# A layer-norm, linear-attention and MLP sum on one core: the MLP pair with the half chunk is moved to the front of the second pass

## The chip, the core and the metric

The kernel runs on one core of a Trainium2 chip. A core has a matrix engine (TensorE, PE in the profile, with PEld for its weight loads), a vector engine (DVE), a scalar engine (ACT), a general engine (POOL) and a queue engine (SP) from which this kernel issues nearly all its transfers; 16 DMA engines move the data. The metric is the device time of one execution in microseconds (us).

## The reference

The input `x` has 2048 tokens of 640 values. Everything is float32.

```python
xn = layernorm(x)
# A: linear attention, 32 heads of 20
q, k, v = split(xn @ wqkv)
phi(z) = concat(softmax(z @ w_phi), softmax(-(z @ w_phi)))      # per head, 40 features
o   = phi(q) @ (phi(k).T @ v) / (phi(q) @ sum(phi(k)) + 1e-6)
A   = o @ wo
# B: MLP, hidden width 1728
B   = gelu(layernorm(xn) @ w1 + b1) @ w2 + b2
out = x + A + B
```

## The kernel before, in words

The tokens are cut into four blocks of 512. A float32 operand is split exactly into a high and a low part, and a product of two operands is three matmuls (`mm3`, lines 69 to 72): high by high, high by low, low by high. The hidden width 1728 is cut into chunks of 128: 13 full ones and a half one of 64. Two chunks make a pair, so there are six full pairs, 0 to 5, and pair 6, which is a full chunk and the half one.

The stages in order of time are:

- The first MLP pass takes all pairs over blocks 0 and 1 (`passes`, line 289). Its sums `acc[0]` and `acc[1]` are stored to `a_dram`.
- The projections of all 16 token tiles, the features of q and k, and the sum over `phi(k)` and `v` (loop at line 1017). The output weights `wo` are split here and stored as `wo_dram`, high and low. The phi of q are stored to `e_dram` (`store_phi`).
- The second MLP pass takes all pairs over blocks 2 and 3. Beside it runs the attention of all four blocks (`attend`, line 1314): its steps are handed out one at a time at each `tick()`, which the code of the MLP calls after each group of matmuls. For a block there are 11 groups of heads, each with a load `e`, a high part on ACT (line 1207), a low part on POOL (1208) and two matmuls (1214, 1215); then `quotients` (line 1235), which stores denominators, loads them as `dt`, takes a reciprocal on DVE (1247), spreads it as `rx` with shuffles on DVE (1263) and multiplies on POOL (1265).
- The output projection (line 1410): 4 blocks x 5 row groups x 15 matmuls. It adds the sums `acc` and stores.

A pair is computed in one of two ways. `passes` takes one block at a time: 15 matmuls per full chunk and block, 10 for the half chunk (whose high and low halves share one weight tile), so 60 for a full pair over two blocks and 50 for pair 6. `cross` (line 414) takes both blocks at once by a scheme with seven block products instead of eight: 7 x 6 matmuls, and 4 x 3 for the fifth slice of the inputs, 54 in all. For it the raw weights are combined on POOL (`sums`), and combined inputs `t2`, `t3`, `t4` lie in `tf0` and `tf1`; the even slices of y[3] are overwritten by `t1`. Inside `cross` the second product of the pair before, `before`, is advanced in five pieces. `second` (line 334) is a pair's second product for one block: five groups of 6 matmuls in three PSUM banks (5, 6, 7), each followed by an add to `acc` on DVE (line 342).

In the second pass before the change pair 0 goes by `passes`, pairs 1 to 5 by `cross`, and pair 6 by `passes` again; for pair 6 the overwritten slices of y[3] are loaded back (line 1385). While pair 6 runs, the output weights are loaded into places `w2` and `w0` (`load_wo`, line 1292), block 0's attention output `ob` into `tf0` and, after it, block 1's into `tf1`, and block 0 is split into high and low parts (`first_split`, line 1301).

The order on TensorE, DVE, ACT and POOL in the second pass is that of the code from line 1358 on; on SP, and on DVE, ACT and POOL before that line, a scheduler sets it when the program is built, and SP issues its transfers in that order and waits before each one for what it needs.

Of the kernel before, what the change touches and what calls it, by code (L numbers as in the profile page):

```python
# [51 lines left out]
def tile_kernel(ctx: ExitStack, tc: tile.TileContext, x, xT, wkT, wqT, wv, wphi, wo, w1, b1, w2, b2,  # L52
# [161 lines left out]
    class Mlp:  # L214
        def __init__(self, slots, hid):
            self.hid, self.turn, self.slots, self.beside, self.raw = hid, 0, slots, iter(()), {}
            self.ph, self.px, self.po = Banks(0, 1, 2), Banks(3, 4), Banks(5, 6, 7)
            self.due, self.ticks = [], 0
# [70 lines left out]
        def passes(self, g, b, ws, hid=None):  # L289
# [7 lines left out]
            for j, (w1h, w1l, w2h, w2l) in enumerate(todo):  # L297
                gt = gts[:, j, :512]
                hs = mtile(self.hid[self.turn][j], F32R)
                hh, hl = hs[:, 0, :512], hs[:, 1, :512]  # L300
                if not (g == 6 and j == 1):
                    self.first(g, j, b, ws[j], gt, hh, hl)
                    hid.append((hh, hl))
                else:
                    pz = self.ph()
                    for kc in range(KC):
                        nc.tensor.matmul(pz, w1h[:, kc, :], yh[:, kc, :], start=kc == 0, stop=False)  # L307
                        nc.tensor.matmul(pz, w1l[:, kc, :], yl[:, kc, :], start=False, stop=kc == KC - 1)  # L308
# [5 lines left out]
                    nc.gpsimd.tensor_tensor(hh[64:128, :], gt[0:64, :], f(hh[0:64, :]), op=ALU.subtract)  # L314
                    hid.append((hh, None))
            yield
            for m in range(KC):
# [10 lines left out]
                if g == 0:  # L328
                    nc.vector.scalar_tensor_tensor(acc[b][:, m, :], pw, b2t[:, m:m + 1], acc[b][:, m, :], op0=ALU.add, op1=ALU.add)
                else:  # L330
                    nc.vector.tensor_tensor(acc[b][:, m, :], pw, acc[b][:, m, :], op=ALU.add)  # L331
# [26 lines left out]
        def take_pair(self, g, second, slot):  # L358
# [158 lines left out]
    mlp = Mlp((0, 1, 2, 3), ((0, 2), (1, 3)))  # L517
# [499 lines left out]
    for t, i in [(t, i) for t in range(14) for i in range(4)] + TAIL:  # L1017
# [35 lines left out]
        if (t, i) == (11, 0):  # L1053
            mlp = Mlp((0, 3, 2, 1), ((1, 2), (0, 3)))
            mlp.ph = ptile
            mlp.fetch_pair(0, False)
        if (t, i) == (12, 3):
            with tc.issue_after(evac):
                w1t, parts = mlp.take_pair(0, False, 0)
                for part in parts:  # L1060
                    part()
            mlp.fetch_pair(0, True)
        if (t, i) == (15, 3):
            w2t, late = mlp.take_pair(0, True, 3)
# [3 lines left out]
    mlp.fetch_pair(1, False)  # L1068
# [33 lines left out]
    before = mlp.passes(0, 2, ws)  # L1102
# [59 lines left out]
    class Attention:  # L1162
# [108 lines left out]
        def split(self, c, eng):  # L1271
# [15 lines left out]
            if c == KC and b < 2:  # L1287

                acc[b] = tfp.tile([P, KC, 512], F32, name=f"tf{b}")
                nc.sync.dma_start(acc[b], a_dram[b])  # L1290

    def load_wo():

        for p, wd in enumerate(wo_dram):
            w = wp.tile([P, 4, D], F32R, name=f"w{(2, 0)[p]}")
            nc.sync.dma_start(f(w), wd[:, 0:4, :])
            last = rp.tile([P, D], F32R, name=f"r{1 + p}")
            nc.sync.dma_start(f(last), wd[:, 4, :])
            wol.append([w[:, kc, :] for kc in range(4)] + [last])
# [37 lines left out]
    with tc.issue_after(subs["q", 15].ins):  # L1337
        mlp.sums(1)
    this = mlp.passes(0, 3, ws)
# [7 lines left out]
    for part in mlp.splits(1):  # L1347
# [3 lines left out]
    mlp.fetch_pair(1, True)  # L1351
# [8 lines left out]
    def gathered(g):  # L1360

        w2t, parts = mlp.take_pair(g, True, 0 if g % 2 else 3)

        def second():
            parts[1]()
            mlp.after(2, lambda: mlp.fetch_pair(g + 1, False))
# [3 lines left out]
    for g in range(1, 6):  # L1370
        w2t, later = gathered(g)
        hid, more = mlp.cross(g, (2, 3), before, later)
        if g < 5:
            parts = mlp.splits(g + 1)
        else:
            w1t, parts = mlp.take_pair(6, False, 1)
# [7 lines left out]
    for p in range(2):  # L1384
        nc.sync.dma_start(f(y[3][p][:, 0:4:2]), y_dram[1][p][:, 0:4:2])
# [5 lines left out]
    w2t, parts = mlp.take_pair(6, True, 3)  # L1391
    ws = pairs(w1t, w2t)
    for b in range(2, 4):
        this = mlp.passes(6, b, ws)
        next(this)
        finish(before)
        before = this
        if b == 2:
            for part in parts:
                part()  # L1400
            mlp.after(8, lambda: load_ob(0))
        else:
            load_wo()
            mlp.beside = both(mlp.beside, first_split())
    finish(before)
    load_ob(1)

    pw_ = Banks(6, 7)
    step = 0
    for b in range(NB):  # L1410
        oh, ol = at[b].oh, at[b].ol
        for m in range(KC):
            ms = slice(m * P, (m + 1) * P)

            for cols in [slice(0, 512)] if (b, m) != (NB - 1, KC - 1) else [slice(0, 256), slice(256, 512)]:
                pw = pw_()[:, cols]
                for c in range(KC):
# [3 lines left out]
                    for n, at_ in enumerate((3, 28, 53), 1):  # L1421
# [67 lines left out]
```

## Time and profile before

| | us |
|---|---|
| median of 3 runs | 713.65 (713.02 to 713.98) |
| the profiled execution | 713.46 |
| its span, first to last instruction | 711.6 |
| PE busy | 703.8 (99%) |
| DVE busy | 514.0 (72%) |
| POOL busy | 421.4 (59%) |
| ACT busy | 342.0 (48%) |
| TensorE clock granted | 1.00 |
| data moved | 106.56 MB, mean 150 GB/s |

An engine's row in a timeline gives the start in us, the length, the engine, the line of the code, the operation, output and inputs by name with their shapes, and in square brackets the idle time before it with what ended it. A row of what TensorE waited for gives the total, the count and the longest wait. Matmul rows overlap, since matmuls are pipelined: the distance between starts is what one costs. In a row of windows stand the stretch, its length, busy time and count for PE, PEld, DVE, ACT and POOL, the granted clock, the busy share of the DMA engines and GB/s.

### The profile page before, as it was taken

To read this page: it belongs to the slowest core of one execution; us is meant where nothing else is said; L and a number is where in the kernel's file an instruction comes from. 1 tells how busy PE (TensorE), PEld (TensorE's weight loads), DVE (VectorE), ACT (ScalarE), POOL (GpSimd) and SP (SyncE) were. 2 spreads that over 40 slices of the span, in tenths; PEclk is the share of its full clock that TensorE was granted. 3 is DMA by queue.
4 is the path that set the end of the run, shared out by engine and by line. 5 is a ranking of instruction groups with operands and counts; after the bars stand their busy time and mean duration, and the time that the engine had idled before them with its cause. 6 is when DMAs were issued, how large, how long until landed. Compare 5 with 4: busy or idle time off the path is not lost. (4 is left out here: it accounts for less than half of the span.)

```text
span 711.6 us, 9745 instructions
## 1 busy us (share of the span) xinstructions
PE 703.8 (99%) x3381; PEld 592.2 (83%) x3381; DVE 514.0 (72%) x821; ACT 342.0 (48%) x563; POOL 421.4 (59%) x360
## 2 busy tenths in 40 slices
PE   9999999999999999999999999999999999999998
PEld 7878888888888888888888888888887878888886
DVE  7777755988754788788888878657769695784622
ACT  6434554444334545545544546367665766450100
POOL 3521314577245997898787879468679787540400
PEclk9999999999999999999999999999999999999999
DMA  9823643485621228236401609964355568446222
GB/s 325 288 72 109 193 121 98 155 266 172 214 105 74 93 75 245 70 110 199 99 0 32 159 1 349 227 191 127 115 162 153 164 187 296 164 127 214 84 80 74
DMA packets 65767, 106.56 MB, mean 150 GB/s; under 512 B 7462, under 2 KB 31814, under 8 KB 63838
## 3 DMA queue, kind: packets, MB, share of 16 engines
q1 hardware_dynamic: 65414, 105.93, 46.5%
q8 instruction: 26, 0.43, 0.2%
q14 instruction: 23, 0.19, 0.1%
q10 hardware_dynamic: 304, 0.01, 0.0%
HBM read 71.37 MB, written 34.55 MB: 149 GB/s over the span
## 5 line engine op out<-in xcount | busy, mean ns | idle before, releaser
L906 PE MATMUL bank<-wkh,y 128*128 128x512 f32 (+1 forms) x480 | 139.5, 364 | 0.0
L70 PE MATMUL bank<-y,w 128*128 128x512 f32 (+1 forms) x294 | 114.2, 389 | 0.0
L71 PE MATMUL bank<-y,w 128*128 128x512 f32 (+1 forms) x294 | 113.7, 387 | 0.0
L72 PE MATMUL bank<-y,w 128*128 128x512 f32 (+1 forms) x294 | 113.6, 386 | 0.0
L64 POOL TENSOR_TENSOR w<-r,w 128x640 fp32r<-128x640 f32 x32 | 52.2, 1645 | 96.0 <-ACT w L61 67.0
L70 PE MATMUL bank<-m,w 128*128 128x512 f32 x260 | 102.3, 394 | 1.1 <-DVE acc L331 0.8
L71 PE MATMUL bank<-m,w 128*128 128x512 f32 x260 | 101.3, 390 | 0.9 <-DVE m L461 0.9
L72 PE MATMUL bank<-m,w 128*128 128x512 f32 x260 | 101.3, 390 | 0.0
L906 PEld LDWEIGHTS bank<-wkh,y 128*128 128x128 f32 x480 | 87.5, 188 | 13.3
L906 PE MATMUL bank<-wkl,y 128*128 128x512 f32 (+1 forms) x240 | 87.4, 364 | 0.0
L70 PEld LDWEIGHTS bank<-y,w 128*128 128x128 f32 x294 | 55.2, 188 | 11.7 <-issue 0.4
L72 PEld LDWEIGHTS bank<-y,w 128*128 128x128 f32 x294 | 55.2, 188 | 11.3
L71 PEld LDWEIGHTS bank<-y,w 128*128 128x128 f32 x294 | 55.2, 188 | 10.9
L942 ACT ACTIVATE m<-m,rs_all 128x1280 f32<-128x1280 f32 x32 | 43.7, 1365 | 42.9 <-POOL m L941 42.8
L70 PEld LDWEIGHTS bank<-m,w 128*128 128x128 f32 x260 | 48.8, 188 | 11.9 <-DVE acc L331 1.0
L944 DVE TENSOR_REDUCE sm<-m 128x64 f32<-128x1280 f32 x32 | 47.4, 1481 | 15.0 <-ACT m L942 14.8
L71 PEld LDWEIGHTS bank<-m,w 128*128 128x128 f32 x260 | 48.8, 188 | 11.1 <-DVE m L461 1.4
L906 PE MATMUL bank<-w,y 128*128 128x512 f32 x240 | 57.4, 391 | 0.0
L72 PEld LDWEIGHTS bank<-m,w 128*128 128x128 f32 x260 | 48.8, 188 | 10.2
L941 POOL TENSOR_TENSOR m<-m,mx 128x640 f32<-128x640 f32 (+2 forms) x48 | 44.4, 939 | 19.2 <-DVE mx L930 19.2
L331 DVE TENSOR_TENSOR acc<-bank,acc 128x512 f32<-128x512 f32 x70 | 46.9, 683 | 11.1 <-PE bank L72 5.9
L906 PEld LDWEIGHTS bank<-w,y 128*128 128x128 f32 x240 | 44.4, 188 | 8.5
(184 smaller groups left out, 1447.2 us busy)
## 6 DMA issues: line engine op xcount, KB each, us to landing
r<-in_w SPq DMA_DIRECT2D x52, 320.0 KB
e<-e SPq DMA_DIRECT2D x40, 256.0 KB
e<-acc SPq DMA_DIRECT2D x52, 160.0 KB
acc<-in_xT SPq DMA_DIRECT2D x4, 1280.0 KB
t<-t SPq DMA_DIRECT2D x8, 512.0 KB
tf<-t SPq DMA_DIRECT2D x2, 1536.0 KB
xb<-in_x SPq DMA_DIRECT2D x8, 320.0 KB
t<-in_x SPq DMA_DIRECT2D x8, 320.0 KB
```

Source lines behind the costliest of these rows:

```text
L64: eng.tensor_tensor(lo, src, f(hi), op=ALU.subtract)
L70: nc.tensor.matmul(ps, lh, rh, start=first, stop=False, **kw)
L71: nc.tensor.matmul(ps, lh, rl, start=False, stop=False, **kw)
L72: nc.tensor.matmul(ps, ll, rh, start=False, stop=last, **kw)
L331: nc.vector.tensor_tensor(acc[b][:, m, :], pw, acc[b][:, m, :], op=ALU.add)
L906: nc.tensor.matmul(ps, lh[:, kc, c], rh[:, kc], start=n == 0, stop=n == 3 * KC - 1)
L941: subs[n, t] = nc.gpsimd.tensor_tensor(ep[:, s], a, b, op=ALU.subtract)
L942: exps[n, t] = nc.scalar.activation(e, e, AF.Exp, scale=rs_all[:, t:t + 1])
L944: nc.vector.tensor_reduce(sm, e.rearrange("p s (h f) -> p (s h) f", f=DH), axis=AX, op=ALU.add)
```

## The change

Pair 6 is put first in the second pass, by `passes`, and pairs 0 to 5 all go by `cross`. So pair 6's weights are fetched and split during the projections, the bias b2 is added in the pass's first pair, whichever it is (`bias`), and y[3] is not loaded back. Pair 6's half chunk now calls `tick()`, in both passes.

At the end the output weights go to places `w0` (high) and `w2` (low), called before and after block 0's `ob`; block 0's saved sum `acc[0]` goes to place `w1`, not to `tf0` after the split; `ob` of block 1 is loaded ahead of the last `second`, and block 0's split is handed out in that. Block 1's split starts at step 8 of the output projection and not at step 3.

```diff
-            self.gelu(g, j, pz, gt, hh, hl, (g, j, b) == (0, 0, 2))
+            self.gelu(g, j, pz, gt, hh, hl, (g, j, b) == (6, 0, 2))
...
                         nc.tensor.matmul(pz, w1l[:, kc, :], yl[:, kc, :], start=False, stop=kc == KC - 1)
+                        self.tick()
...
                         nc.tensor.matmul(pw, w2l[:, ms], hh, start=False, stop=True)
-                if g == 0:
+                        self.tick()
+                if g == self.bias:
...
-                if 0 < g < 6:
+                if g < 6:
                     return self.split(hi, lo, r)
...
-            mlp.fetch_pair(0, False)
+            mlp.fetch_pair(6, False)
...
-            w2t, late = mlp.take_pair(0, True, 3)
+            w2t, late = mlp.take_pair(6, True, 3)
             late.pop(0)()
     with tc.issue_after(subs["q", 15].ins):
         late.pop()()
-    mlp.fetch_pair(1, False)
+    mlp.fetch_pair(0, False)
...
-    before = mlp.passes(0, 2, ws)
+    before = mlp.passes(6, 2, ws)
...
             if c == KC and b < 2:
-                acc[b] = tfp.tile([P, KC, 512], F32, name=f"tf{b}")
-                nc.sync.dma_start(acc[b], a_dram[b])
...
+                if b:
+                    acc[b] = tfp.tile([P, KC, 512], F32, name=f"tf{b}")
+                    nc.sync.dma_start(acc[b], a_dram[b])
+
+    def load_wo(p):
+
+        w = wp.tile([P, 4, D], F32R, name=f"w{(0, 2)[p]}")
+        nc.sync.dma_start(f(w), wo_dram[p][:, 0:4, :])
+        last = rp.tile([P, D], F32R, name=f"r{1 + p}")
+        nc.sync.dma_start(f(last), wo_dram[p][:, 4, :])
+        wol.append([w[:, kc, :] for kc in range(4)] + [last])
...
-        w2t, parts = mlp.take_pair(g, True, 0 if g % 2 else 3)
+        w2t, parts = mlp.take_pair(g, True, 3 if g % 2 else 0)
...
-    for g in range(1, 6):
+    for g in range(5):
...
-    for p in range(2):
-        nc.sync.dma_start(f(y[3][p][:, 0:4:2]), y_dram[1][p][:, 0:4:2])
...
-    w2t, parts = mlp.take_pair(6, True, 3)
-    ws = pairs(w1t, w2t)
-    for b in range(2, 4):
-        this = mlp.passes(6, b, ws)
-        next(this)
-        finish(before)
-        before = this
-        if b == 2:
-            for part in parts:
-                part()
-            mlp.after(8, lambda: load_ob(0))
-        else:
-            load_wo()
-            mlp.beside = both(mlp.beside, first_split())
-    finish(before)
+    w2t, later = gathered(5)
+    hid, more = mlp.cross(5, (2, 3), before, later)
+    load_wo(0)
+    load_ob(0)
+    load_wo(1)
+    for _ in mlp.second(5, 2, w2t, hid[0]):
+        next(more, None)
+    acc[0] = wp.tile([P, 4, D], F32, name="w1").rearrange("p i d -> p (i d)").rearrange("p (c t) -> p c t", c=KC)
+    nc.sync.dma_start(acc[0], a_dram[0])
     load_ob(1)
+    mlp.beside = both(mlp.beside, first_split())
+    finish(mlp.second(5, 3, w2t, hid[1]))
...
-                    for n, at_ in enumerate((3, 28, 53), 1):
+                    for n, at_ in enumerate((8, 28, 53), 1):
```

Three places show how instructions move. Lines of the changed kernel are two to nine off those of before. First SP at the start of the second pass, before: `r` are raw weights of the next pair, `y` the overwritten slices of y[3], `e_73` the stored phi of block 3, `e` the attention's loads.

```order
L356 DMA r_4112<-in_w 128x640
L1345 DMA y_3061<-t_86 128x512
L1345 DMA y_3060<-t_86 128x512
L1009 DMA e_73<-acc_2045 32x10x128 x8
L1009 DMA e_73<-et 32x10x128 x4
L1009 DMA e_73<-acc_2044 32x10x128 x4
L1345 DMA y_3060<-t_87 128x512
L1345 DMA y_3061<-t_87 128x512
L354 DMA r_4367<-in_w 128x640
L354 DMA r_4368<-in_w 128x640
L1176 DMA e<-e_70 80x512
```

The same place in the changed kernel:

```order
L358 DMA r_4116<-in_w 128x640
L1347 DMA y_3060<-t_86 128x512
L1347 DMA y_3061<-t_86 128x512
L1347 DMA y_3060<-t_87 128x512
L1347 DMA y_3061<-t_87 128x512
L1011 DMA e_73<-acc_2045 32x10x128 x8
L1011 DMA e_73<-et 32x10x128 x4
L1011 DMA e_73<-acc_2044 32x10x128 x4
L356 DMA r_4360<-in_w 128x640
L356 DMA r_4361<-in_w 128x640
L1178 DMA e<-e_70 80x512
```

All four loads of `y` now stand ahead of the 16 stores of phi; the attention's first load stays behind stores and raw weights.

Second SP at the end, before: `woh` and `wol` are the high and low output weights, `d_98` and `dt` belong to block 3's quotients, `a_90` is block 0's saved sum.

```order
L1296 DMA w_5989<-wol 128x2560
L1298 DMA r_5991<-wol 128x640
L1298 DMA r_5987<-woh 128x640
L1240 DMA d_98<-acc_5547 4x2560
L1240 DMA d_98<-acc_5547 2x2560
L1244 DMA acc_5547<-o_83 4x2560
L1242 DMA dt<-d_98 128x128
L1244 DMA acc_5547<-o_83 4x2560
L1290 DMA tf_6023<-a_90 128x2560
L1248 DMA d_99<-dt 128x128
```

The same place in the changed kernel:

```order
L1300 DMA r_5942<-woh 128x640
L1387 DMA tf_5944<-ob_88 128x2560
L1300 DMA r_5948<-wol 128x640
L1387 DMA tf_5998<-ob_89 128x2560
L1242 DMA d_98<-acc_5535 4x2560
L1242 DMA d_98<-acc_5535 2x2560
L1397 DMA w_5996<-a_90 128x2560
L1298 DMA w_5946<-wol 128x2560
L1298 DMA w_5940<-woh 128x2560
L1246 DMA acc_5535<-o_83 4x2560
L1244 DMA dt<-d_98 128x128
L1250 DMA d_99<-dt 128x128
```

Both `ob`, the saved sum and both weights now stand ahead of the load of `dt`.

Third DVE at the end, before: L331 are the adds of pair 6's second product, L1286 the low parts of the attention output, L1424 the output projection's adds.

```order
L331 TENSOR_TENSOR acc_4123<-bank_6016,acc_4123 128x512
L331 TENSOR_TENSOR acc_4123<-bank_6028,acc_4123 128x512
L331 TENSOR_TENSOR acc_4123<-bank_6035,acc_4123 128x512
L1247 RECIPROCAL dt<-dt 128x128
L1286 TENSOR_TENSOR y_6055<-tf_6042,y_6054 128x512 x2
L1424 TENSOR_TENSOR tf_6023<-bank_6044,tf_6023 128x512
```

In the changed kernel L344 are the adds of pair 5's second product, `acc_4126` for block 2 and `acc_4127` for block 3, and L463 the low parts of its hidden tiles for block 3:

```order
L344 TENSOR_TENSOR acc_4126<-bank_5959,acc_4126 128x512
L463 TENSOR_TENSOR m_5938<-m_5768,m_5938 128x512
L1249 RECIPROCAL dt<-dt 128x128
L344 TENSOR_TENSOR acc_4126<-bank_5968,acc_4126 128x512
L344 TENSOR_TENSOR acc_4126<-bank_5979,acc_4126 128x512
L463 TENSOR_TENSOR m_5939<-m_5768,m_5939 128x512
L344 TENSOR_TENSOR acc_4126<-bank_5988,acc_4126 128x512
L1288 TENSOR_TENSOR y_6005<-tf_5944,y_6004 128x512 x3
L344 TENSOR_TENSOR acc_4127<-bank_6000,acc_4127 128x512
```

The reciprocal stood behind all adds of the second pass and stands now between the second and the third add of the last pair's block 2.

More of the change, by code (lines that the diff above doesn't have):

```diff
@@ L214, in tile_kernel, with __init__ @@
     class Mlp:
-        def __init__(self, slots, hid):
-            self.hid, self.turn, self.slots, self.beside, self.raw = hid, 0, slots, iter(()), {}
+        def __init__(self, slots, hid, bias):
+            self.bias, self.hid, self.turn, self.slots, self.beside, self.raw = bias, hid, 0, slots, iter(()), {}
             self.ph, self.px, self.po = Banks(0, 1, 2), Banks(3, 4), Banks(5, 6, 7)
@@ L1287, in split @@
             if c == KC and b < 2:
-                acc[b] = tfp.tile([P, KC, 512], F32, name=f"tf{b}")
[L1290 to L1299, printed above, removed]
+                if b:
[7 more added lines that the diff above has]
+        wol.append([w[:, kc, :] for kc in range(4)] + [last])
     def first_split():
@@ L1337, in tile_kernel @@
     with tc.issue_after(subs["q", 15].ins):
-        mlp.sums(1)
-    this = mlp.passes(0, 3, ws)
+        mlp.sums(0)
+    this = mlp.passes(6, 3, ws)
     next(this)
@@ L1346, in tile_kernel @@
     mlp.places()
-    for part in mlp.splits(1):
+    for part in mlp.splits(0):
         part()
```

18 lines of the change are left out of this document (8 added, 10 removed).

## The prediction

> **What bounds the kernel now.** I read the page's busy shares first, then what TensorE waited for, then the second MLP pass and the end on the queues of SP, DVE and ACT.
>
> ```profile
> PE 703.8 (99%) x3381; PEld 592.2 (83%) x3381; DVE 514.0 (72%) x821; ACT 342.0 (48%) x563; POOL 421.4 (59%) x360
> ```
>
> ```profile
> PE bank L71 <- DVE m L461: 0.9, 1, 0.9
> ...
> PE bank L1214 <- DVE acc L1228: 0.6, 1, 0.6
> ```
>
> ```profile
> 458.84 0.39 PE L70 MATMUL bank<-y,w 128*128 128x512 f32 x1
> ...
> 469.04 0.39 PE L70 MATMUL bank<-tf,w 128*128 128x512 f32 x1
> ...
> 471.76 0.39 PE L70 MATMUL bank<-y,w 128*128 128x512 f32 x1
> ...
> 639.76 0.47 PE L70 MATMUL bank<-y,w 128*128 128x512 f32 x1
> ```
>
> TensorE is busy 703.8 of 711.6 us, and in the whole second pass it waits twice, 0.9 and 0.6 us. The row at 458.84 opens the first seven-product pair, 469.04 is its fifth product (s3 by t3), 639.76 opens the output projection. From 469.04 to 471.76 stand 12 matmuls: 2.72 us, 0.227 us each (the 0.39 us of a row overlap). So every matmul removed is worth 0.227 us, and every new wait counts in full. What has to be asked is which loads and engine queues were just early enough.
>
> **Matmuls removed.** A pair in two plain blocks has 60 first matmuls, by seven products 54. Pair 0 changes to seven products: 6 fewer, nothing else on TensorE: 6 x 0.227 = **-1.36 us**. No other instruction of it is added.
>
> **The first seven-product pair comes earlier.** Ahead of it stand now 25 + 25 + 25 matmuls of pair 6 instead of 30 + 30 + 30 of pair 0, and inside it, up to s3 by t3, three pieces of 5 instead of 6. TensorE would be there 18 x 0.227 = 4.1 us sooner, at 469.04 - 4.08 = 464.96 on the old clock. What is late there is a transfer:
>
> ```profile
> 447.03 5.20 SPq L1009 DMA_DIRECT2D e<-acc  x8
> ...
> 458.38 0.91 SPq L1345 DMA_DIRECT2D y<-t  x2
> 459.72 0.81 SPq L354 DMA_DIRECT2D r<-in_w  x2
> 460.64 0.36 SPq L1176 DMA_DIRECT2D e<-e  x1
> ```
>
> ```profile
> 428.00:444.00 16.00, 16.00 (x83) 13.56 (x82) 12.46 (x17) 10.89 (x16) 15.57 (x17) 1.00 0.97 369
> 444.00:448.00 4.00, 4.00 (x20) 3.30 (x19) 4.00 (x12) 1.62 (x4) 1.57 (x3) 1.00 0.75 270
> 448.00:460.00 12.00, 12.00 (x84) 10.71 (x83) 8.77 (x18) 4.43 (x8) 7.37 (x6) 1.00 0.98 221
> 460.00:468.00 8.00, 8.00 (x37) 6.64 (x36) 2.26 (x4) 3.82 (x7) 1.61 (x2) 1.00 0.99 282
> ...
> 604.00:608.00 4.00, 4.00 (x19) 3.30 (x19) 3.98 (x7) 1.80 (x4) 1.67 (x2) 1.00 1.03 404
> ```
>
> ```profile
> 467.37 0.63 ACT L1207 ACTIVATE m<-e 128x512 fp32r<-128x512 f32 x1 [1.12 <-DMA e<-e]
> 467.91 0.58 ACT L449 ACTIVATE m<-bank 128x512 f32<-128x512 f32 x1
> ```
>
> The last two figures of a window's row are the DMA share and GB/s. From 428 to 468 the transfers are the bound of their own chain: share 0.97 to 0.99, but for 0.75 in 444 to 448. The first attention rows (`e`) land last in it: ACT waits 1.12 us for them until 467.37. Behind that copy on ACT stands L449, which empties bank `a` (end 468.49), and s3 by t3 may write the bank only then; TensorE came at 469.04, 0.55 us later. The order of the changed kernel keeps these two ACT instructions in that place. The bytes ahead of `e` stay too (`acc`, `tf`, two raw weights, `y`, the phi stores, two raw weights); only the `y` loads move ahead of the stores. They can fill the gap of 444 to 448, worth 0.25 x 4 = 1 us. Against it stand the stores, which wait for DVE and POOL:
>
> ```profile
> 446.50 0.90 DVE L1003 STREAM_TRANSPOSE acc<-m 128x320 f32<-128x320 f32 x2
> ```
>
> ```profile
> 617.08 1.29 POOL L314 TENSOR_TENSOR m<-m,m 64x512 fp32r<-64x512 f32 x1 [3.58 <-DMA r<-in_w]
> ```
>
> ```profile
> 623.06 0.59 DVE L370 MEMSET w<- 64x640 f32 x1 [0.19 <-issue]
> 624.26 1.67 DVE L371 TENSOR_TENSOR w<-r,w 64x640 fp32r<-64x640 f32 x1 [0.61 <-ACT w L369]
> ```
>
> The first store left at 447.03, as the transposes of 446.50 were done. Ahead of these DVE now has the half chunk's memset (0.59), its subtraction (up to 1.67) and an add, and POOL a subtraction of 1.29 that waits for ACT: I take 1.5 us later, about where the moved `y` loads (2 x 2 x 256 KB) end. So `e` lands between 466.3 (all of the 1 us won) and 468.8 (none won, 1.5 lost); I take 466.8, the middle of the won microsecond, since the `y` loads fill what the stores leave. The bank is free 1.12 us later, at 467.9: TensorE **waits 3.0 us** here in sum (part of it may show a few microseconds earlier, at the second matmuls of pair 6, which wait for POOL's 1.29; that wait comes out of the same 3.0). Ends: nothing, if the rows come 3 us sooner, and 5.0 (`e` at 468.8).
>
> The half chunk's other work (w1 split under the projections, DVE 72% busy; ticks added in the first pass) lies beside a TensorE that never waited there: 0, and at most the 0.9 us of a wait like L461's. Taking pair 6 from the end removes two `y` reloads of 512 KB and DVE work: 0 on the path.
>
> **Pair 5 by seven products with block 2's quotients.** In before the quotients of blocks 0 and 1 (shuffles on a full DVE) met a seven-product pair, and there lie the two waits of 0.9 and 0.6 us; block 2's met pair 6 with no wait. Now these meet pair 5. Ends 0 and 0.9; I take **+0.4**, the middle, as neither is nearer.
>
> **The end.** Count back from the first output-projection matmul, at which TensorE would be if it never waited: zero. `tf0` comes free 92 matmuls before, -20.9 us; places `w1`, `w2`, `w0` 75, 66 and 60 matmuls before: -17.0, -15.0, -13.6. SP issues in this order: `ob0` to tf0, 320 KB, `ob1` to tf1, `a0` to w1, the low and the high output weights to w2 and w0 (5 x 1280 KB + 320 KB = 6.88 MB), and behind them the load of `dt`, 64 KB, for block 3's quotients. DVE's reciprocal of `dt` now stands after the second add of `second(5, 2)`, ahead of three adds, a hidden tile's low part and block 0's split. In before it stood after all of pair 6's adds.
>
> ```profile
> 594.25 0.38 SPq L1389 DMA_DIRECT2D tf<-ob  x1
> ...
> 596.41 1.24 SPq L1389 DMA_DIRECT2D tf<-ob  x1
> ...
> 598.49 0.34 SPq L1248 DMA_DIRECT2D d<-dt  x1
> ...
> 602.07 0.32 SPq L1296 DMA_DIRECT2D w<-woh  x1
> ...
> 607.03 0.53 SPq L1252 DMA_DIRECT2D rx<-d  x1
> ...
> 631.55 0.44 SPq L1242 DMA_DIRECT2D dt<-d  x1
> ...
> 639.09 0.32 SPq L1290 DMA_DIRECT2D tf<-a  x1
> ```
>
> ```profile
> 638.97 1.88 DVE L331 TENSOR_TENSOR acc<-bank,acc 128x512 f32<-128x512 f32 x3
> 640.77 0.94 DVE L1247 RECIPROCAL dt<-dt 128x128 f32<-128x128 f32 x1
> ...
> 644.82 0.69 DVE L1424 TENSOR_TENSOR tf<-bank,tf 128x512 f32<-128x512 f32 x1 [1.97 <-DMA tf<-a]
> ```
>
> In before `dt` left at 631.55 into an empty queue and DVE used it at 640.77 with no wait. A small transfer behind large ones is seen at 598.49: 64 KB behind the 1280 KB of 594.25 and 596.41; `rx`, which needs it, left at 607.03, 8.5 us later. One load of 1280 KB alone took 644.82 - 639.09 = 5.7 us; at the 404 GB/s of 604 to 608 its bytes are 3.3, so 2.4 are fixed. Now: -20.9 + 0.2 + 6.88 MB / 404 GB/s (17.0) + 2.4 + 0.2 for dt's own bytes: `dt` lands at -1.1, say -1.0. Until then DVE stands. `second(5, 2)` has three banks: it runs out at -6.8 (30 matmuls ahead of zero). After the landing DVE needs 0.9 for the reciprocal and 3 x 0.6 (1.88 for three) for two adds and the low part: block 3's fifth matmul goes at +1.75, and 26 matmuls, 5.9 us, follow, with 0.25 for banks that the split holds: +7.9. The output projection starts **7.9 us late**. The weights are there by then: they and the split cost nothing more. The slowest and the fastest busy stretch give the ends:
>
> ```profile
> 596.00:600.00 4.00, 4.00 (x20) 3.30 (x19) 2.88 (x6) 2.45 (x5) 1.55 (x2) 1.00 0.90 331
> ...
> 436.00:443.00 7.00, 7.00 (x38) 5.94 (x37) 3.46 (x6) 5.25 (x7) 6.61 (x9) 1.00 1.04 433
> ```
>
> At 331 GB/s `dt` lands at 2.7 and the term is +11.6; at 433 it lands at -2.2, +6.7.
>
> The Trainium skill, "DMA: Bandwidth & Descriptors", Queues, rings and completion order, says that each DMA engine takes the descriptors of one ring in order, and SP has one ring on each; the 8.5 us agree. With the fabric ceiling that its Specifications give, 435 GB/s, an estimate of the term is +6.6 instead of 7.9.
>
> **Sum.** 713.46 (the profiled execution: span 711.6 and 1.9 around it) - 1.36 + 3.0 + 0.4 + 7.9 = **723.4**. The median of the three runs is 0.19 above the profiled time, so I say 723.6.
>
> **The rivals.**
> 1. *Small transfers are not held back by large ones.* Then `dt` lands some 2.6 us after its issue at about -12.7, at -10, before DVE needs it, and `e` (256 KB behind the stores) lands 3 us sooner: neither wait. 713.46 - 1.36 = 712.1, with 0.4 of pair 5 712.5: not slower. It decides from the point where `dt` lands before -8.6 (-6.8 + 0.9 for four matmuls - 2.75 on DVE). Against it: 598.49 to 607.03. Chance 0.08. The Trainium skill, same page and section, says too that completion on one queue is not in order, so that a later small transfer may end first, which is this rival's way; the 8.5 us speak against that here.
> 2. *Only the start is hit*: SP gets to `dt` before the weights, as their places come free late; end 0, 713.46 - 1.36 + 3.0 + 0.4 = 715.5; if then the high weights come at 331 GB/s, they land at 2.5 instead of -1.3, and zero is held 2.5 us: 718.0. For it: SP's order is only reached if every wait ahead comes early. Against it: `dt` stands behind both weights in the order itself. Chance 0.12.
> 3. *Only the end is hit*: `e` comes in time, 720.4. The DMA share of 0.98 speaks against it. Chance 0.09.
> 4. *More than said*: slow transfers at the end (+11.6) with `e` at 468.8: 713.46 - 1.36 + 5.0 + 0.4 + 11.6 = 729.1. Chance 0.07.
> 5. The change may not do what it says if seven products did not remove matmuls; the order has six fewer, so it gets no chance.
>
> My forecast has 0.64.
>
> **How the numbers follow.** 0.2% is 1.4 us, about what a measurement of this kernel can tell from no change. Faster by more (below 712.2): 0.04, the half of rival 1 in which one of the two old waits goes as well. Within: 0.07, its other half and 0.03 of rival 2's low end. Slower: 0.89. The forecast's own range is 719.5 to 727.5 (end term 6.7 to 11.6, start 1.5 to 5.0, not both at an end); to leave out no more than 2 in 10 the range takes in rival 3 and the upper half of rival 2 (0.64 + 0.09 + 0.06): 716.5 to 728.
>
> **What would show it.** Right: DVE's reciprocal of `dt` with 6 to 10 us idle before it, put down to the load; TensorE with one wait of 5 to 8 us at a second matmul of pair 5 behind DVE; ACT waiting for `e` with TensorE's s3 by t3 behind L449; 3375 matmuls. Wrong: a reciprocal without a wait; a TensorE wait on the output weights instead; a first pair that starts its s3 product before 466 on the old clock. The forecast is wrong most easily by the time at which the three places come free, and by the queue's rate there.

## The result and the profile after

The changed kernel takes 725.91 us (median of 5 runs, 725.13 to 728.32) where the kernel before takes 713.98 on the same chip: 1.0179 times, 95% interval 1.0161 to 1.0198. The forecast was 723.6, range 716.5 to 728.0. The profiled execution took 728.32 us, 14.86 more than that of before; where these 14.86 us lie is read from its trace.

First the page's line of busy times and what TensorE waited for (engine, line, released by: us in total, times, longest).

```profile
PE 708.2 (97%) x3375; PEld 593.8 (82%) x3375; DVE 521.5 (72%) x826; ACT 344.9 (47%) x568; POOL 426.2 (59%) x364
```

```profile
PE bank L70 <- DVE acc L344: 7.9, 1, 7.9
PE bank L70 <- ACT m L451: 2.0, 1, 2.0
PE bank L307 <- DVE v L972: 1.4, 1, 1.4
...
PE bank L1216 <- DVE acc L1230: 0.6, 1, 0.6
```

There are 6 matmuls fewer, as said. Three waits are new: 7.9, 2.0 and 1.4 us. The old wait of 0.9 us behind DVE's `m L461` is gone, the other old one (0.6) stays. The lines of the changed kernel are up to 2 higher than those of before here, 6 lower from the output projection on. On TensorE's own timeline (start, duration, operation, and in brackets the idle time before it):

```profile
437.78 0.47 PE L307 MATMUL bank<-y,w 128*128 128x512 f32 x1 [1.39 <-DVE v L972]
...
469.96 0.50 PE L70 MATMUL bank<-tf,w 128*128 128x512 f32 x1 [1.97 <-ACT m L451]
...
645.16 0.77 PE L70 MATMUL bank<-m,w 128*128 128x512 f32 x1 [7.94 <-DVE acc L344]
...
654.91 0.39 PE L70 MATMUL bank<-y,w 128*128 128x512 f32 x1
```

The first is the half chunk's first matmul, the second s3 by t3 of the first seven-product pair, the third opens `second(5, 3)`, the last opens the output projection. It comes 15.15 us later than in before (639.76), so everything was lost ahead of it.

The chain behind the long wait, on DVE and on SP:

```profile
643.52 0.95 DVE L1249 RECIPROCAL dt<-dt 128x128 f32<-128x128 f32 x1 [9.04 <-DMA dt<-d]
644.39 1.22 DVE L344 TENSOR_TENSOR acc<-bank,acc 128x512 f32<-128x512 f32 x2
```

```profile
625.24 1.11 SPq L1242 DMA_DIRECT2D d<-acc  x2
...
630.46 0.32 SPq L1298 DMA_DIRECT2D w<-woh  x1
633.01 0.54 SPq L1246 DMA_DIRECT2D acc<-o  x1
633.65 0.39 SPq L1244 DMA_DIRECT2D dt<-d  x1
```

DVE stands 9.04 us for `dt`. `dt` passes the loaded DMA engines twice: its values are stored to `d` at 625.24 and SP can issue what needs them at 633.01, 7.8 us later; the load leaves at 633.65 and is used at 643.52, 9.9 us later. The two passes lie beside the same large loads, all of which had been issued by 630.46: the packets of `dt` (512 bytes each) moved only from 641.04 to 642.72, and from 633.0 to 641.1 the engines were busy at 424 GB/s. So `dt` came when the bytes ahead of it were through. In before the same store took 2.4 us, with the engines busy for 38% of that time:

```profile
628.60 1.16 SPq L1240 DMA_DIRECT2D d<-acc  x2
630.99 0.52 SPq L1244 DMA_DIRECT2D acc<-o  x1
```

The chain behind the two waits at the start, on DVE, POOL, SP and ACT:

```profile
433.11 2.12 DVE L373 TENSOR_TENSOR w<-r,w 64x640 fp32r<-64x640 f32 x1
...
436.78 0.86 DVE L972 SCALAR_TENSOR_TENSOR v<-bank,rs_all,v 128x480 fp32r<-128x480 f32 x2
```

```profile
446.66 1.29 POOL L315 TENSOR_TENSOR m<-m,m 64x512 fp32r<-64x512 f32 x1 [4.52 <-DVE m L64]
```

```profile
450.19 5.34 SPq L1011 DMA_DIRECT2D e<-acc  x8
```

```profile
468.79 0.63 ACT L1209 ACTIVATE m<-e 128x512 fp32r<-128x512 f32 x1 [1.11 <-DMA e<-e]
469.33 0.58 ACT L451 ACTIVATE m<-bank 128x512 f32<-128x512 f32 x1
```

DVE splits the half chunk's `w2` (a memset of 0.59 us at 432.48, then the row of 2.12) ahead of L972, which empties the projection's bank that the half chunk's first matmul needs. POOL stands 4.5 us for the half chunk's low part (L315) with the last features behind it; the first phi store leaves at 450.19, not 447.03; `e` is there at 468.79, not 467.37; and the L451 copy of 469.33, on which s3 by t3 waits, stands behind it.

Last, stretches of the trace (length, then busy us of PE, PEld, DVE, ACT, POOL with counts, the granted clock, DMA share and GB/s):

```profile
466.93:470.34 3.41, 1.44 (x7) 0.89 (x6) 1.46 (x2) 2.30 (x5) 2.39 (x2) 1.00 0.96 319
470.34:473.76 3.42, 3.42 (x10) 2.66 (x9) 0.00 (x0) 1.83 (x4) 3.19 (x3) 0.50 0.60 209
...
637.60:641.01 3.41, 0.00 (x0) 0.00 (x0) 0.00 (x0) 0.00 (x0) 0.00 (x0) 1.00 1.01 423
641.01:644.42 3.41, 0.00 (x0) 0.00 (x0) 0.90 (x2) 0.00 (x0) 0.00 (x0) 0.50 0.21 73
644.42:647.84 3.42, 2.68 (x6) 2.15 (x7) 3.42 (x7) 0.00 (x0) 0.00 (x0) 0.50 0.10 31
647.84:651.25 3.41, 3.41 (x9) 2.64 (x8) 3.16 (x6) 0.00 (x0) 0.00 (x0) 0.50 0.07 24
651.25:654.66 3.41, 3.41 (x16) 2.82 (x15) 1.49 (x3) 0.00 (x0) 0.00 (x0) 1.00 0.00 0
```

This was not foreseen at all: after the 2.0 us wait and in the 7.9 us wait the granted clock falls to 0.5, and a busy stretch of 3.41 us then holds 9 or 10 matmuls instead of 16. In before the clock was 1.00 from 6 us on, up to the last matmuls.

The account of the 14.86 us of the profiled execution:

| term | us | from |
|---|---|---|
| six matmuls fewer | -1.36 | 6 x 0.227 |
| old wait behind L461 gone | -0.95 | the waits of before |
| TensorE is later in the first pass and the projections | +0.90 | the last v projections but one open at 431.54 (L978) and 430.64 (L976 of before); the wait of 0.22 at 154.71 is the only one of it that shows |
| half chunk's first matmul | +1.39 | row at 437.78 |
| s3 by t3 | +1.97 | row at 469.96 |
| half clock behind it | +1.7 | half of 470.34 to 473.76 |
| start of `second(5, 3)` | +7.94 | row at 645.16 |
| half clock behind it | +3.0 | half of 645.16 to 651.25 |

The two half-clock terms are estimates. The sum is 14.6; the rest is 0.3.

### The profile page after: what moved, and what is told of

It is laid out like the page before. It is cut to its first block, busy times and chain, and to the rows that moved or that the text cites. A ratio compares the mean times of both kernels' runs of the same rounds, so it can differ in the third digit from the quotient of the medians.

```text
span 726.5 us, 9734 instructions
## 1 busy us (share of the span) xinstructions
PE 708.2 (97%) x3375; PEld 593.8 (82%) x3375; DVE 521.5 (72%) x826; ACT 344.9 (47%) x568; POOL 426.2 (59%) x364
## 4 chain that ended last, share of the span: by engine, by line
PE 74%; DVE 7%; POOL 6%; DMA 5%; issue 4%; SPq 2%; ACT 2%; ACTq 0%; POOLq 0%; DVEq 0%
PE bank L908 21%; PE bank L70 15%; PE bank L72 15%; PE bank L71 15%; POOL w L64 2%; POOL m L943 2%; PE bank L646 2%; PE bank L978 2%; DMA r<-in_w 1%; DMA dt<-d 1%; PE bank L1216 1%; SPq L1011 1%; PE bank L1217 1%; POOL m L954 1%; DMA d<-acc 1%
## 5 line engine op out<-in xcount | busy, mean ns | idle before, releaser
L70 PE MATMUL bank<-m,w 128*128 128x512 f32 x260 | 103.8, 399 | 9.3 <-DVE acc L344 7.9
L70 PE MATMUL bank<-y,w 128*128 128x512 f32 (+1 forms) x286 | 111.1, 388 | 0.0
L71 PE MATMUL bank<-y,w 128*128 128x512 f32 (+1 forms) x286 | 110.5, 386 | 0.0
L72 PE MATMUL bank<-y,w 128*128 128x512 f32 (+1 forms) x286 | 110.5, 386 | 0.0
L64 POOL TENSOR_TENSOR w<-r,w 128x640 fp32r<-128x640 f32 x28 | 45.9, 1655 | 97.0 <-ACT w L61 68.0
L71 PE MATMUL bank<-m,w 128*128 128x512 f32 x260 | 102.4, 394 | 0.0
L72 PE MATMUL bank<-m,w 128*128 128x512 f32 x260 | 102.2, 393 | 0.0
L70 PEld LDWEIGHTS bank<-m,w 128*128 128x128 f32 x260 | 49.5, 190 | 21.6 <-issue 8.3
L72 PEld LDWEIGHTS bank<-y,w 128*128 128x128 f32 x286 | 53.7, 188 | 11.1
L70 PEld LDWEIGHTS bank<-y,w 128*128 128x128 f32 x286 | 53.7, 188 | 10.9
L71 PEld LDWEIGHTS bank<-y,w 128*128 128x128 f32 x286 | 53.7, 188 | 10.7
L72 PEld LDWEIGHTS bank<-m,w 128*128 128x128 f32 x260 | 49.5, 190 | 10.6
L71 PEld LDWEIGHTS bank<-m,w 128*128 128x128 f32 x260 | 49.6, 191 | 10.1 <-DVE m L463 0.2
L344 DVE TENSOR_TENSOR acc<-bank,acc 128x512 f32<-128x512 f32 x60 | 40.7, 683 | 15.4 <-PE bank L72 14.9
```

The lines of the kernel that those rows point to most:

```text
L64: eng.tensor_tensor(lo, src, f(hi), op=ALU.subtract)
L70: nc.tensor.matmul(ps, lh, rh, start=first, stop=False, **kw)
L71: nc.tensor.matmul(ps, lh, rl, start=False, stop=False, **kw)
L72: nc.tensor.matmul(ps, ll, rh, start=False, stop=last, **kw)
```

## The experiments

The theory to be tested has three parts: DVE stands for `dt`, which is late behind the large loads of SP's queue; at the start ACT's copy stands behind `e`; and, new after the result, an idle TensorE has its clock halved and pays for that. Times are medians, ratios are to the kernel before on the same chip.

**The reciprocal later on DVE.**

```diff
-            for i in range(13):
+            for i in range(13 if self.b < 3 else 31):
                 yield
             nc.vector.reciprocal(dt, dt)
```

> Block 3's reciprocal of `dt` stands 18 steps later: behind the last add of `second(5, 3)` on DVE instead of ahead of the third add of `second(5, 2)`. No load is moved. Theory (DVE stands in order for `dt`, TensorE runs out of banks): TensorE's wait of 7.9 us behind DVE L344 is gone, and with it the stretch at clock 0.5 that followed it (1.5 to 2.9 us), so 725.9 goes to 715 to 716.5. Rival (the output weights or block 0's split are what is late, and the reciprocal only stands in front of them): the wait moves to the first output-projection matmul, of 3 to 8 us, and the time stays at 720 or above.

Measured: 716.78 us, 1.0045 (1.0028 to 1.0063). DVE's reciprocal and TensorE's first matmul of the output projection:

```profile
643.02 0.94 DVE L1249 RECIPROCAL dt<-dt 128x128 f32<-128x128 f32 x1
```

```profile
642.21 0.39 PE L70 MATMUL bank<-y,w 128*128 128x512 f32 x1
```

TensorE has no wait from 580 us to the end, the clock is 1.00 throughout, and the reciprocal finds `dt` there. The loads are the same, so the output weights and the split were not late: the rival falls. Some 9.6 us, three quarters of the loss (1.0179 to 1.0045 times 714), hang on the place of this one instruction among DVE's.

**The small transfers on another queue.**

```diff
+            que = nc.gpsimd if self.b == 3 else nc.sync
...
-                nc.sync.dma_start(den[r].rearrange(form, q=q), ob[30 + i::128 // q])
+                que.dma_start(den[r].rearrange(form, q=q), ob[30 + i::128 // q])
...
-            nc.sync.dma_start(dt, den.rearrange("h (q t) -> (h q) t", q=4))
+            que.dma_start(dt, den.rearrange("h (q t) -> (h q) t", q=4))
```

> The two stores to `d` and the load of `dt` of block 3 are issued by POOL, which has no other work there, instead of SP; every other load and DVE's order stay. Theory (`dt` is late because it stands behind the large loads in SP's queue, twice: its stores and then itself): `dt` lands before DVE comes to it at about 634.5, the reciprocal waits under 1 us, TensorE does not wait there, 715 to 716.5. Rival (the transfers share one fabric, so a small one is as late from any queue, or SP's order was not the cause): the reciprocal still waits 5 us or more, 722 or above.

Measured: 723.78 us, 1.0152 (1.0121 to 1.0182). POOL, DVE, and the list of transfers (KB, us from issue to landing) of the stretch 624 to 640:

```profile
624.85 1.27 POOL L1243 DMA_DIRECT2D d<-acc  x2
632.71 0.58 POOL L1245 DMA_DIRECT2D dt<-d  x1 [6.59 <-DMA d<-acc]
```

```profile
638.58 0.95 DVE L1250 RECIPROCAL dt<-dt 128x128 f32<-128x128 f32 x1 [5.86 <-DMA dt<-d]
```

```profile
DMA packets 908, 6.55 MB, mean 410 GB/s; under 512 B 163, under 2 KB 163, under 8 KB 307
...
dt<-d POOLq DMA_DIRECT2D x1, 64.0 KB, 5.8
...
d<-acc POOLq DMA_DIRECT2D x1, 40.0 KB, 6.8
```

The theory's number failed. On a queue of their own the store still takes 6.8 us and the load 5.8. TensorE's wait falls from 7.9 to 4.8 us only. So moving the small transfers out of SP's queue takes 3.2 us off the wait, not all of it, while the same engines move 410 GB/s. The packets of POOL's queue, which holds nothing else, show where the time goes: the store is issued at 624.85, its first data packet moves at 629.06 and its last ends at 630.9; the load is issued at 632.71, its 16 packets move from 636.46 to 637.7. So 4.2 and 3.75 us pass before any packet moves, and the packets themselves need 1.8 and 1.2 us beside SP's loads. What fills the time before them, POOL's way of issuing or the busy engines, is not shown by this run. The Trainium skill, "DMA: Bandwidth & Descriptors", Queues, rings and completion order, says that an engine takes turns between its queues, a packet at a time. The 1.2 us of the load's packets agree with that; the 3.75 us ahead of them are not explained by it.

**Two large loads behind `dt`.**

```diff
-            nc.sync.dma_start(dt, den.rearrange("h (q t) -> (h q) t", q=4))
+            self.seen = nc.sync.dma_start(dt, den.rearrange("h (q t) -> (h q) t", q=4))
...
-    load_ob(1)
     mlp.beside = both(mlp.beside, first_split())
     finish(mlp.second(5, 3, w2t, hid[1]))
+    with tc.issue_after(at[3].seen.ins):
+        load_ob(1)
```

> `ob1` is issued behind `dt`, and with it SP's order puts the high output weights behind `dt` too; DVE's order stays. Ahead of `dt` stand now `ob0`, 320 KB twice, `a0` and the low weights, 2.6 MB less than in the changed kernel. Theory (the bytes ahead of `dt` set its landing): 2.6 MB at 420 GB/s are 6.1 us, and the stores to `d` land sooner as well, so of the 7.9 us wait 0 to 1.8 are left; 715 to 718.5. Rival (the place of the reciprocal alone costs, whatever the queue holds): still 6 us or more of wait, 723 or above. A third way, the high weights now come late: a wait at the first output-projection matmul, put down to a load.

Measured: 723.02 us, 1.0129 (1.0102 to 1.0157). SP and DVE, and two stretches of this run:

```profile
629.32 0.60 SPq L1244 DMA_DIRECT2D dt<-d  x1
```

```profile
638.83 0.95 DVE L1249 RECIPROCAL dt<-dt 128x128 f32<-128x128 f32 x1 [5.28 <-DMA dt<-d]
```

```profile
629.00:633.00 4.00, 4.00 (x20) 3.30 (x19) 2.12 (x4) 4.00 (x8) 0.00 (x0) 1.00 0.95 323
...
636.00:638.00 2.00, 0.30 (x2) 0.00 (x0) 0.00 (x0) 0.00 (x0) 0.00 (x0) 1.00 1.06 186
```

`dt` leaves 4.3 us sooner than in the changed kernel (629.32 for 633.65), and the wait falls from 7.9 to 4.2 us, not to 0 to 1.8; neither theory's number. The load still takes 9.5 us, with 2.6 MB fewer ahead of it. The bytes ahead did not go at 420 GB/s: 323 from 629 to 633, and 186 from 636 to 638 with all engines busy. By the packets of 512 bytes in the trace, `dt`'s first moved at 634.98, 96 of its 128 were through by 636.3, and the last 32 moved from 637.49 to 638.23; between 636 and 638 a 10 KB packet of the large loads took 0.9 us in the median, where it took 0.39 from 633 to 636. Why these stretches are slow stays open. The bytes ahead matter, but they are a poor clock.

**The wait filled with matmuls.** The products go to a spare bank and are read by nothing.

```diff
+    spare = banks.tile([P, 512], F32, name="bank0")
+    for i in range(34):
+        nc.tensor.matmul(spare, w2t[:, 0, 0:P], hid[0][0][0], start=True, stop=True)
     finish(mlp.second(5, 3, w2t, hid[1]))
```

> 34 matmuls of 512 columns into a spare bank, read by nothing, stand between `second(5, 2)` and `second(5, 3)`, where TensorE waits 7.9 us; all else stays. They take 34 x 0.227 = 7.7 us. Theory (the clock is halved because TensorE stood idle): DVE waits for `dt` as long as before, TensorE goes on at the same moment, but the granted clock is 1.0 all the way, so the 1.5 to 2.9 us of half-speed matmuls go: 723 to 724.4. Rival (the clock drops for another reason, such as the transfers at 430 GB/s): the clock of 0.5 is still seen in 641 to 651, and the time stays at 725.9 or grows.

Measured: 726.04 us, 1.0173 (1.0156 to 1.0189). The clock stayed at 1.00, yet the time was not below the changed kernel's, which had run in another comparison; the start had cost this run more (2.7 us at s3 by t3). So both were run again side by side, the changed kernel as it is.

> The changed kernel as it is, beside the run with the filled wait on the same chip. Both theories of the clock expect 725.9 (1.0179 times before) and a clock of 0.5 for 6.8 to 13.7 us; it is there to be compared with.

> The filled wait once more, beside the changed kernel. Theory (an idle TensorE has its clock halved, and that costs): granted clock 1.0, and 1.0 to 2.9 us less than the changed kernel in this call. Rival (the half clock costs nothing, as DVE or the loads hold the end anyway): the clock is 1.0 and the time is that of the changed kernel within 0.5 us.

Measured: the changed kernel 727.06 us, 1.0184 (1.0161 to 1.0206); with the wait filled 725.64 us, 1.0155 (1.0131 to 1.0179). Stretches of the changed kernel, then of the filled one:

```profile
637.00:645.00 8.00, 1.79 (x4) 1.50 (x5) 3.43 (x6) 0.00 (x0) 0.00 (x0) 0.63 0.34 134
645.00:653.00 8.00, 8.00 (x28) 6.36 (x27) 5.54 (x9) 0.00 (x0) 0.00 (x0) 0.73 0.05 15
```

```profile
637.00:645.00 8.00, 8.00 (x36) 6.33 (x34) 0.78 (x1) 0.00 (x0) 0.00 (x0) 1.00 0.64 264
645.00:653.00 8.00, 7.17 (x30) 5.40 (x30) 7.92 (x14) 0.00 (x0) 0.00 (x0) 1.00 0.08 24
```

With TensorE kept busy over the same wait the clock does not fall there: the idleness makes it fall, since the loads were the same. From the first matmul after the wait to the end of the span both profiles of the changed kernel need 81.3 and 81.4 us (726.5 less 645.16; 724.6 less 643.21), both of the filled one 79.1 and 79.0 (724.4 less 645.33; 724.9 less 645.87): the half clock costs 2.3 us at the end. By the whole times it is 1.4 us here, in the expected 1.0 to 2.9, with intervals that still overlap, since the start varies by as much.

**The attention's first copy 3 steps later on ACT.** This and all that follow stand on the late reciprocal.

```diff
-                yield from at[b].groups(10 if b == 0 else 0, 2, (2,), 2)
+                yield from at[b].groups(13 if b == 0 else 0, 2, (2,), 2)
```

> On top of the late reciprocal (716.78, 1.0045 times before): the attention's first copy L1209, which waits for `e`, stands 3 steps later, so that on ACT the copy of bank `a` (L451) for s3 by t3 comes ahead of it. No load is moved. Theory (the bank waits behind ACT's copy of `e`, not for its own matmuls): TensorE's wait behind ACT m L451, 1.3 to 2.7 us in the runs so far, falls to 0.4 or less, and the time by 0.9 to 2.3 us, to 1.0015 to 1.0030. Rival (`e` is late for whoever comes first): the wait moves to the first attention product L1216 or to the next copy of the bank, and the time stays at 1.0045.

Measured: 714.81 us, 1.0014 (1.0006 to 1.0023). TensorE's waits:

```profile
PE bank L1216 <- DVE acc L1230: 1.5, 1, 1.5
...
PE bank L70 <- ACT m L451: 0.5, 1, 0.5
```

The wait at s3 by t3 is 0.5 where it was 1.3, and the ratio falls by 0.0031, some 2.2 us. No load was moved, so the bank did wait behind ACT's copy of `e`. An old wait later in the pass (L1216) has 1.5 us instead of 1.1, so a little comes back. These rows account for 0.4 of the 2.2 us, and the two profiled executions differ by 0.1 us of span (713.8 and 713.7); the late reciprocal alone had 4 runs, on another chip. So the cause of the wait is shown, and how much time the edit gives is not.

**The half chunk's `w2` split behind the last v copies.**

```diff
-    with tc.issue_after(subs["q", 15].ins):
+    with tc.issue_after(evac):
         late.pop()()
```

> On top of the late reciprocal: the split of the half chunk's `w2` (ACT L371, DVE L373, 2.1 us) is issued behind the last v copies, so that DVE empties the projection's bank (L972) first. Theory (half chunk's memset and subtraction on DVE ahead of L972 hold the bank): TensorE's wait of 1.4 us at the half chunk's first matmul (L307) is gone, to under 0.3, and the time falls by 1.1 to 1.4 us, to 1.0025 to 1.0030. Rival (what is won there is waited for again): the subtraction now stands ahead of DVE's transposes, the phi stores go later, `e` lands later, and TensorE waits the same microsecond more at s3 by t3; 1.0045.

Measured: 715.86 us, 1.0027 (1.0016 to 1.0038), the theory's number, but the trace does not bear the theory out:

```profile
446.87 0.50 PE L71 MATMUL bank<-m,w 128*128 128x512 f32 x1 [0.59 <-DVE m L64]
...
448.19 0.50 PE L327 MATMUL bank<-m,w 128*128 128x512 f32 x1 [0.58 <-POOL m L315]
```

The wait at L307 is gone, and 1.2 us of its 1.4 are waited for 9 us later: TensorE is now ahead of the hidden rows of pair 6. At s3 by t3 it waits 1.8 us where it was 1.3, as the rival had it. So these rows do not explain the lower ratio. DVE's split did hold the bank; the gain was not there to be had.

**The half chunk's low part on DVE.**

```diff
-                    nc.gpsimd.tensor_tensor(hh[64:128, :], gt[0:64, :], f(hh[0:64, :]), op=ALU.subtract)
+                    (nc.vector if self.bias else nc.gpsimd).tensor_tensor(hh[64:128, :], gt[0:64, :], f(hh[0:64, :]), op=ALU.subtract)
```

> On top of the late reciprocal: in the second pass the half chunk's low part (L315) is made by DVE instead of POOL, which stood 4.5 us for it ahead of the last features (L997, L999). Theory (POOL's stand is what delays the phi stores, and they delay `e`): the first phi store leaves 2 to 3 us sooner than at 450.2, `e` lands 1 us sooner or more, and the wait at s3 by t3 falls to 0.8 or less; 1.0020 to 1.0040. Rival (the transfers themselves bound `e`, share 0.98): the store leaves sooner, `e` lands when it did, within 0.4 us; 1.0045.

Measured: 714.79 us, 1.0012 (1.0001 to 1.0022). SP and TensorE:

```profile
449.30 5.34 SPq L1011 DMA_DIRECT2D e<-acc  x8
```

```profile
468.80 0.50 PE L70 MATMUL bank<-tf,w 128*128 128x512 f32 x1 [0.96 <-ACT m L451]
```

With the late reciprocal alone the store left at 450.37, `e` was there at 468.27 and the wait was 1.3 us. The store is 1.1 us sooner, not 2 to 3, `e` 0.6 (467.63), the wait 0.3 shorter. The direction is the theory's, the size is a third of it. The time fell by more than these rows account for (0.0033, with intervals that allow 0.0006).

**All of these, and no ticks in the first pass's half chunk.** The three edits above, and at both places of the half chunk:

```diff
-                        self.tick()
+                        if self.bias:
+                            self.tick()
```

> The late reciprocal, the three edits of the start together, and no `tick` in the half chunk of the first pass (as in before). Theory (each wait was named rightly and they add up): 6 matmuls fewer, 1.36 us, the old wait of 0.95 gone, nothing new but up to 1 us: 711.3 to 713 where before is 713.5, 0.9970 to 0.9995. Rival (a wait removed is waited for again later, as transfers set the pace): one of the waits at L307, L451 or L1216 of 1 us or more is left, 1.0000 to 1.0030.

Measured: 716.21 us, 1.0028 (1.0017 to 1.0039): worse than two of its parts alone. TensorE and two stretches (this kernel's lines are 1 higher than the changed one's here):

```profile
449.00 0.63 PE L328 MATMUL bank<-m,w 128*128 128x512 f32 x1 [1.25 <-DVE m L316]
```

```profile
445.81:449.22 3.41, 1.59 (x6) 0.70 (x5) 3.35 (x6) 1.20 (x3) 2.56 (x4) 1.00 1.01 375
449.22:452.63 3.41, 3.41 (x9) 2.64 (x9) 3.41 (x7) 2.95 (x5) 1.06 (x1) 0.50 0.67 132
```

DVE, which now has the low part (L316) beside the full chunk's (L64) and the `w2` split, holds TensorE 0.57 and 1.25 us at 447 to 449, and behind these two short waits in one stretch comes the half clock, by estimate 1.7 us more. By the granted clock, 5 of the 10 runs had such a stretch. Edits that each help do not add up when two of them load the same engine. A wait of 0.60 at 155 is still there, so the ticks do not explain the first pass, and what does stays open.

**Late reciprocal, late first copy, low part on DVE; then the `w2` split on POOL as well.** The first leaves the `w2` split where the change put it; the second adds:

```diff
-                    nc.vector.memset(f(lo[64:128, :]), 0.0)
-                    nc.vector.tensor_tensor(lo[0:64, :], r[0:64, :], f(hi[0:64, :]), op=ALU.subtract)
+                    nc.gpsimd.memset(f(lo[64:128, :]), 0.0)
+                    with tc.issue_after(exps["q", 15].ins):
+                        nc.gpsimd.tensor_tensor(lo[0:64, :], r[0:64, :], f(hi[0:64, :]), op=ALU.subtract)
```

> Late reciprocal, late first copy of the attention and the half chunk's low part on DVE, without the edit of the `w2` split. Theory (the run with all edits lost 1.9 us since its early matmuls met hidden rows that were not ready, with a half-clock stretch behind that; without that edit the others add up): no wait at 447 to 449, under 0.3 at s3 by t3, 1.4 left at L307: 713.6 to 714.6, 0.9995 to 1.0008. Rival (those two edits remove the same wait, so one is enough): 1.0010 to 1.0015, as each alone.

> As the run before it, and the half chunk's `w2` memset and subtraction are made by POOL, behind the last features, in the time in which it stood waiting for L315; DVE is 2.7 us freer, and L972 comes at once. Theory (DVE's 2.7 us are what both the bank at L307 and the hidden rows wait for): neither wait is left, 712.2 to 713.4, 0.9975 to 0.9995. Rival (the hidden rows of pair 6 hang on ACT's table load and copies, not on DVE): 1.4 us are won at L307 and 1 us or more is waited for again at 447 to 449: 1.0000 to 1.0015.

Measured: 714.21 us, 1.0004 (0.9992 to 1.0017), then 713.79 us, 0.9995 (0.9983 to 1.0007). TensorE in the second:

```profile
446.69 0.50 PE L327 MATMUL bank<-m,w 128*128 128x512 f32 x1 [0.66 <-DVE m L315]
...
579.01 0.50 PE L1217 MATMUL bank<-m,kvs 128*128 128x512 f32 x1 [1.49 <-DVE acc L1231]
```

The first has 1.38 us left at L307 and 0.65 at s3 by t3, where under 0.3 was expected. In the second neither wait is there; 0.66 of the 1.4 us is waited for again at the hidden rows, and the attention's wait has grown from 0.6 to 1.5. So with the waits at L307, at s3 by t3 and at the end removed the kernel is as fast as before, not faster: of the 2.3 us that six matmuls and the old wait behind L461 had given, 1.5 go to these two waits (0.66, and 1.49 less 0.6), and the other 0.8 lie within the interval. No version tried beats the kernel before by more than the measurement can tell.

## Why the prediction was right, and where it was off

- *Six matmuls, -1.36.* As said: 3375 matmuls, and no wait in pair 5 up to the one at the end.
- *The start, +3.0.* The mechanism was right: s3 by t3 waits behind L449 (now L451), which stands behind ACT's copy of `e`; moving that copy alone takes most of the wait away. The row shows 1.97 us, 1.3 to 2.7 in the other runs that leave the start as it is. But counted as the prediction counts, from 464.96, the row at 469.96 is 5.0 us late, which is the upper end that it gave for `e` at 468.8; `e` was there at 468.79, not at 466.8. So the term was mis-sized, by the landing of `e`. What failed in it is "I take 1.5 us later" for the stores: POOL's stand of 4.5 us was read as a short one, and the first store left 3.2 us later, of which 0.9 came from ahead. Of the 5.0 us, 3.0 show before s3 by t3: 0.9 ahead of the second pass, 1.39 at L307, the rest in short gaps.
- *"0, and at most the 0.9 us" for the half chunk's other work.* Wrong: its `w2` split on DVE holds the bank at L307 for 1.39 us. I had charged these 2.7 us of DVE to the stores and not to the bank that the next copy on DVE empties. Since `e` set the time of s3 by t3, they are part of the 5.0 us and not on top of them.
- *Pair 5 with block 2's quotients, +0.4.* Measured 0, and the old 0.95 went too. The step took old waits as the price of a meeting that had none here.
- *The end, +7.9.* The wait is 7.94 us, and the reciprocal is the cause, as the first experiment shows; the weights and the split cost nothing. The path was right too: SP issued into the four places at -20.8, -17.0, -14.9 and -13.6 us where -20.9, -17.0, -15.0 and -13.6 were said (zero is the unwaited start of the output projection, 637.23 + 30 x 0.227 = 644.0), and `dt` came when the bytes ahead of it were through, 0.5 us ahead of zero where 1.0 was said. That the store to `d` also took 7.8 us was not foreseen, but by this reading it cost nothing, as the loads ahead were still moving when it was done. That 7.94 is so near to 7.9 is in part luck: `dt` came 0.5 us later, and TensorE needed one add of DVE before its next matmul and had 30 left, where three operations and 26 matmuls were counted. That SP's order alone makes `dt` late is not shown: another queue took 3.2 us off the wait, fewer bytes ahead 3.7.
- *Rival 1, small transfers are not held back*, falls by the 7.8 and 9.9 us. Rivals 2 and 3 fall since both places were hit. Rival 4 (729.1) has nearly the time of the profiled execution, for another reason.
- *What the sum did not have:* the half clock, 1.7 and 3.0 us in the profiled execution (2.3 of the latter by comparison). The prediction counted every wait with its length alone. With the 0.9 us ahead of the second pass this covers what lies between 723.4 and the 728.3 of the profiled execution. Three of the five runs of the changed kernel have a granted clock of 0.993, as 10.24 us at half speed give, and take 725.1 to 725.9 us; two, the profiled one among them, have 0.990, as 13.65 us give, and take 727.7 and 728.3. So the median run, by its clock, had the half clock at the end alone.

## What to carry to other kernels

Before a small operation that needs a round trip through memory is moved in an in-order engine's list, ask what stands behind it there: here one reciprocal of 0.95 us held adds, the adds held banks, and TensorE lost some 9.6 us, which came back when it stood 18 steps later. A wait on TensorE can cost more than its length, when the clock falls behind it; count the matmuls of the next stretches at half speed when more than about half of 3.4 us goes idle. An edit that removes a wait is worth only the distance to the next thing that is not ready, so try edits together before adding up what each gained alone.

## What the runs showed of the hardware

The 2.7 us wait in the first run with the filled wait falls on two of the clock's steps; the first of them is:

```profile
466.32:469.74 3.42, 2.01 (x9) 1.32 (x8) 1.50 (x2) 1.22 (x2) 1.06 (x1) 1.00 1.01 305
```

The stretch with the wait of 1.8 us at s3 by t3 in the run with the late `w2` split, and the one behind it:

```profile
468.42:471.83 3.41, 1.84 (x8) 1.54 (x9) 0.55 (x1) 2.40 (x5) 2.88 (x3) 1.00 0.94 345
471.83:475.25 3.42, 3.42 (x17) 2.84 (x16) 0.69 (x1) 1.36 (x3) 3.02 (x3) 1.00 0.30 100
```

- The granted clock changes on a raster of 3.41 us: the stretches at 0.5 between the first matmuls and the last are 3.41, 6.83 or 10.24 us long in all runs that have one. A stretch in which TensorE was busy 1.44 or 1.59 of 3.41 us was followed by one at 0.5; one with 1.84 of 3.41 and one with 2.01 of 3.42 were not. So the same wait halves the clock or not by where it falls: 1.97 us did, 1.93, 2.20 and 2.68 us in other runs did not. At the half clock, a stretch that is busy 2.68 of 3.42 us is followed by another at 0.5, a full one by 1.00. The Trainium skill, "TensorE: Matmul & The Clock Gate", What's actually happening, has the free-running window of some 3.4 us, which the trace agrees with; it asks for a whole idle window before the clock falls, and here less than 60% of one was enough.
- A 64 KB load, and a 40 KB store ahead of it, took 9.9 and 7.8 us beside transfers at 407 to 424 GB/s, and 5.8 and 6.8 us from a queue with nothing else in it, of which 3.75 and 4.2 us passed before their first packet moved.
